# Two post-processing steps, a fetch and three orders moved in an attention and GEGLU kernel

## The chip, the cores and the metric

The kernel runs on one core of one Trainium2 chip. The metric is the device time in microseconds of one execution of the program; lower is better. Engines are called by their names in the profile: PE is TensorE (PEld its weight loads), DVE is VectorE, ACT is ScalarE, POOL is GpSimd and SP is SyncE, which here only issues DMAs.

## The reference

The input x has 2048 rows (S) of 576 columns (D); the GEGLU's inner width is 4608 (F). All data is fp32.

```python
xn = layernorm(x)
q, k, v = heads(xn @ wqkv)              # 32 heads of 18 columns
pq, pk = phi(q), phi(k)                 # where(t > 0, t + 1, exp(t)) + 1e-6
o = (pq @ (pk.T @ v)) / (pq @ sum(pk) + 1e-6)     # linear attention, no mask
s = o @ wo
h = gelu(xn @ w_gate) * (xn @ w_up)     # 2048 x 4608
out = x + s * silu(h @ w_down)
```

## The kernel before, in words

Every fp32 operand of a matmul is split into two words that TensorE takes at full rate: a high word, written by ACT as a rounding copy, and a low word, which DVE makes by subtracting the high word from the source. A product then takes three matmuls (high by high, and the two mixed ones). The large products use a Strassen-like scheme, so that fewer block products are multiplied and DVE and POOL add blocks instead. All instructions are issued in the order in which the Python program runs; nothing reorders them. The helpers `act`, `vec`, `mm`, `pool` and `dma` (lines 145 to 157) issue one instruction each, so L146 is any ACT instruction, L149 any of DVE, L152 any matmul, L155 any of POOL and L158 any DMA.

The stages are these.

- **k, v and q.** `kv_tile(t)` (line 582) makes k and v of tile t of 128 rows in three passes (`x_mm(t, 0..2)`); between them it post-processes k (`k_post`: DVE takes `e_k` and `pk` from PSUM, ACT the exponential, POOL the sum) and v (`v_post`: ACT copies to `va`), and it normalises tile t+1 for the matmuls (`place(t + 1)`: DVE subtracts `mr` from `x` and makes `xf`, ACT makes the high word `xo`, DVE the low word). Tile 8 is N0, the first of the second half of the rows; q of the rows in between is made in `q_mm` and `q_store` (ACT `e_q`, DVE `ph`, POOL the sum of both). A table of hooks names what runs beside each piece. `sort_rows(n)` transposes the layernorm statistics on PE and copies them to `mr` with one ACT instruction.
- **Attention output.** `s_mm` multiplies by the state; `den`, `scale` and `halve` make the denominators, the scaled `pq` and its words, piece by piece in a table of hooks.
- **Gate and up.** 36 matrices (18 of gate, 18 of up) of seven block products each, named al, be, ga, de, al, ga, de. `step` (line 1007) issues each product in two halves and runs the post-processing of an earlier product behind it; so the last two posts, `post_5` (reads ga) and `post_6` (reads de), are left over at the end, and `flush()` (line 1020) issues the last half product and then both. A post adds to u, stores to a spot of SBUF (`spot_g`, `spot_h`, `spot_m`) and runs what the list `todo` hangs on it; POOL adds up combinations of h from those spots (`run_events`) and they go to `hs` in DRAM. At the gate's start the x operands `B21`, `B22` and `T4` come back from DRAM by `back` on SP's queue, with the second weight matrix (`load_mat(1)`, tile `raw_1`) between.
- **Down.** 26 block products p of h words and w_down words, five units each (`UNITS`: two blocks of 128 rows of K in each, one in the last). A block is 12 matmuls of 128x288, so that a unit of two is 24. `load_unit` fetches h words from `hs` into `raw_a`, `raw_b`, `raw_h`, `raw_g`; `cut(u)` (line 1260) splits unit u: ACT writes the high word to `hi` or `beside`, DVE overwrites the raw tile with the low word. `make_words` splits w_down's block into `w_head` (five blocks of K) and `w_end` (four). `down_all` (line 1460) cuts two units ahead of the matmuls: `cut(u + 2)` stands ahead of the matmuls of unit u. The cuts of units 0 to 2 and the words of product 0 hang on the last posts (`down_first`, line 1440): `post_5` of the last up matrix carries `cut(2)` and the second half of product 0's words. The high word of unit 3 goes into the part of `hi` that unit 0's matmuls read. After a product, `read` adds its PSUM banks (`bd`) to the accumulators (`acc`); an output that is complete is closed by `close` (line 1406), per tile of 128 rows one silu on ACT, two DVE additions or products on `sx`, and a store. The list `late` of closings is worked off two a unit. The last product runs tile by tile, with `add_in` on DVE ahead of it.

```python
if u:
    cut(u + 2)
for kt in range(*UNITS[k]):
    down_mm(p, kt, range(TT))
load_unit(p + 1, k)
```

Of the kernel before, what the change touches and what calls it, by code (L numbers as in the profile page):

```python
# [16 lines left out]
P = 128  # L17
S = 2048
D = 576
# [3 lines left out]
HALF = D // 2  # L23
# [4 lines left out]
NG = DF // (2 * P)  # L28
# [28 lines left out]
NM = NG // 2  # L57

KP, TP = (1, 0, 2, 3), (3, 1, 2, 0)
# [43 lines left out]
def block_kernel(ctx, tc, x, xe, xt, wq_d, wkv_d, wo, wgu_d, wd_d, out):  # L103
    nc = tc.nc
# [473 lines left out]
    def run(todo, n=None):  # L578
        for _ in range(len(todo) if n is None else min(n, len(todo))):
            todo.pop(0)()  # L580

    def kv_tile(t, late_=(), end=()):

        ahead = t % (2 * TT) != 2 * TT - 1
        x_mm(t, 0)
        if t % 2 == 0:
            kv_pair(t)
        n0 = (t + 1) // 2 * 2
        if n0 in mixed:
            sort_rows(n0)  # L590
        if ahead:
            turn(t + 1)
        k_post(t, 0)
        x_mm(t, 1)
        if ahead:
            place(t + 1)
            save(t + 1)
        k_post(t, 1)
        v_post(t, 1)
        run(list(late_))  # L600
        x_mm(t, 2)
        run(list(end))
        v_post(t, 2)

    def kv_pair(t):

# [45 lines left out]
    at = {}  # L652
# [366 lines left out]

    def flush():  # L1020
        phase(True, begun_.pop())
        for f in posts:
            f()
        posts.clear()
# [67 lines left out]
    spots, free, place_of, left, events = [], {}, {}, {}, {}  # L1092
# [57 lines left out]
    def run_events(at):  # L1150
        for f in events.pop(at, []):
            f()
# [56 lines left out]
    def load_reg(at, nm, third=None):  # L1209
        if at not in reg:  # L1210
            b = big(REG[at], [P, ODD_W if REG[at] in ODD else REG_W], F32, f"b_{at}")
            reg[at] = b[:, 0 : KT * HALF].rearrange("p (k d) -> p k d", k=KT)
        j, c = int(nm[0]) - 1, int(nm[1]) - 1
        par, f = divmod(KP[j], 2)
        src = wd_d[par::2, :, f, c * HALF : (c + 1) * HALF].rearrange("g p d -> p g d")
        k = slice(0, KT) if third is None else slice(3 * third, 3 * third + 3)
        dma(out=reg[at][:, k], in_=src[:, k])

# [236 lines left out]
    def closings(p):  # L1455
        return [
            lambda o=o, j=j: close(o, j) for o, e in ENDS.items() if e == p for j in range(TT)
        ]

    def down_all():  # L1460
        late = []
        last = NP - 1
        for u in range(NP * NU):
            p, k = divmod(u, NU)
            n = KT * p + 2 * k
            for at in sorted(events):
                if at <= H_END + n // 2:
                    run_events(at)
            if p in LOADS and k < 3:
                load_reg(*LOADS[p], k)  # L1470
            if k == 0:
                for o, e in ENDS.items():
                    if e == p:
                        load_sx(o)
            if k < 2:
                change(p + 1, k)
                if p in SHARED:
                    make_words(p + 1, k)
            elif k < 4:
                make_words(p + 1, k - 2)  # L1480
                if p + 1 in SHARED and p:
                    make_words(p + 2, k - 2)
            if p == last and k == 0:
                read(p - 1)
                late += closings(p - 1)
            if p == last and k == 1:
                run(late, 1)
            if u:
                cut(u + 2)
            if p == last and k == 2:  # L1490
                break
            for kt in range(*UNITS[k]):
                down_mm(p, kt, range(TT))
            load_unit(p + 1, k)
            run(stores)
            if p == last:
                continue
            if k == 1 and p:
                read(p - 1)
                late += closings(p - 1)  # L1500
            else:
                run(late, 2)
        run(late)
        run(stores)
        o = next(o for o, e in ENDS.items() if e == last)
        for j in (TT - 2, TT - 1):
            add_in(o, j, last)
        for j in range(TT):
            for kt in range(UNITS[2][0], KT):
                down_mm(last, kt, (j,))  # L1510
            late += close_last(o, j, last, j >= TT - 2)
            run(late, len(late) - 1)
        run(late)
# [166 lines left out]
    def form_apart(nm):  # L1680
# [16 lines left out]
        (0, 1): [lambda: scales(N0), lambda: form("T1")],  # L1697
        (0, 2): [lambda: form_apart("T3")],
        (0, 3): [lambda: turn(N0)],
        (1, 0): [lambda: place(N0)],  # L1700
        (1, 1): [lambda: form("T2"), lambda: spread(N0 + 2, 2), lambda: scales(N0 + 2)],
    }
# [4 lines left out]
    for n in range(N0, 2 * N0):  # L1707
# [12 lines left out]
            ends.append(make_sel)  # L1720
        if n == 2 * N0 - 1:
            ends += [lambda i=i: difference(1, i) for i in range(3)]
        kv_tile(n, late_, ends)
    ahead = {
        (2, 0): [
            lambda: kv_pair(2 * N0), kv_done, lambda: q_hold(2, 7, 4), spread_sel,
# [3 lines left out]
        (2, 2): [lambda: kv_wo(0), lambda: kv_wo(1), move_rows],  # L1730
        (2, 3): [lambda: kv_wo(2), lambda: kv_wo(3)],
        (3, 0): [lambda: den(2), lambda: q_hold(3, 8, 4)],
        (3, 1): [lambda: scale(2, 0, 1), lambda: halve(2, 0, 1)],
        (3, 2): [lambda: scale(2, 2, 3), lambda: halve(2, 2, 3)],
        (3, 3): [lambda: scale(2, 4), lambda: halve(2, 4)],
    }
    for tb in (2, 3):
        for gi in range(NHG - 1):
# [41 lines left out]
    wt["last"] = sb.tile([P, 2, P], F32R, tag="small", bufs=1, name="w_last")  # L1780
    back("T3")
    run(pieces[4] + pieces[5])
    back("B21", eng=nc.sync)
    load_mat(1)
    back("B22", "T4", eng=nc.sync)
    open_spots()
    for q in range(NQ):
        g = q // 2
# [72 lines left out]
```

## Time and profile before

| | us |
|---|---|
| median of 3 runs | 1441.13 |
| lowest and highest of the runs | 1439.12, 1441.52 |
| the profiled execution, whole | 1439.22 |
| its span in the profile | 1437.5 |
| PE busy in it | 1429.8 (99%) |
| DVE busy | 1009.7 (70%) |
| ACT busy | 578.8 (40%) |
| POOL busy | 539.3 (38%) |

The span runs from the first to the last instruction of the profiled execution; 1.7 us of that execution lie outside it. Busy times are sums over the whole span; matmuls are pipelined, so that a start of one lies before the end of the one ahead. Times of rows are counted from the span's start. In the names of tiles `bd` is PSUM of down, `raw_*` the h words and then their low words, `hi` and `beside` their high words.

### The profile page before, as it was taken

The numbers are of one execution on the slowest core, as the hardware profiler recorded it, in microseconds if no ns is written. First come the engines' busy times: TensorE is split into PE (matmuls) and PEld (weight loads), VectorE is DVE, ScalarE is ACT, GpSimd is POOL, SyncE is SP. The second block draws the span as 40 slices with busy tenths as digits, with TensorE's granted clock in tenths as the row PEclk, the third lists the DMA queues.
The fourth block names the chain that finished last, engine by engine and source line by source line (L and its number), as shares of the span: only waits on it lengthen the run. The fifth ranks groups of instructions, "written<-read, shape, count | busy, mean of one in ns | idle before, by whom it ended". The sixth has DMA issues, their size and how long they took to land.

```text
span 1437.5 us, 29286 instructions
## 1 busy us (share of the span) xinstructions
PE 1429.8 (99%) x11656; PEld 1386.1 (96%) x11656; DVE 1009.7 (70%) x1519; ACT 578.8 (40%) x1249; POOL 539.3 (38%) x550
## 2 busy tenths in 40 slices
PE   9999999999999999999999999999999999999998
PEld 8989989999999999999999999999999999999998
DVE  7778667354766756566655766656678978989898
ACT  6354365333322333322333322333336455545444
POOL 3342340125756557565465755557432000000000
PEclk9999999999999999999999999999999999999999
DMA  5454105521423314233242332314289888767886
GB/s 218 169 190 163 45 21 206 193 90 57 167 85 113 119 56 169 89 122 118 73 144 75 131 116 103 128 60 162 78 291 365 260 260 254 242 194 228 284 287 224
DMA packets 120947, 228.16 MB, mean 159 GB/s; under 512 B 11658, under 2 KB 45354, under 8 KB 120170
## 3 DMA queue, kind: packets, MB, share of 16 engines
q1 hardware_dynamic: 118234, 216.13, 44.4%
q0 software_dynamic: 2432, 9.96, 1.9%
q8 instruction: 92, 1.51, 0.5%
q14 instruction: 45, 0.37, 0.1%
q10 hardware_dynamic: 144, 0.20, 0.1%
HBM read 144.93 MB, written 81.27 MB: 157 GB/s over the span
## 4 chain that ended last, share of the span: by engine, by line
PE 93%; DVE 4%; DMA 1%; ACT 1%; issue 1%; SPq 0%; POOL 0%; ACTq 0%; DVEq 0%; POOLq 0%
PE bd L152 22%; PE ga L152 17%; PE al L152 15%; PE de L152 15%; PE kv L152 8%; PE be L152 7%; PE s L152 4%; PE q L152 2%; DMA raw_h<-hs 1%; PE kv_a L152 1%; DVE xo_T L149 1%; DVE raw_h L149 0%; PE idle L152 0%; DVE w_end L149 0%; PE d L152 0%
## 5 line engine op out<-in xcount | busy, mean ns | idle before, releaser
L155 POOL TENSOR_TENSOR sums<-raw 128x256 f32<-128x256 f32 (+1 forms) x108 | 70.5, 652 | 159.2 <-DMA raw<-in_wgu_dram 132.8
L152 PE MATMUL de<-xo_T,wa 64*128 64x512 f32 x486 | 127.4, 386 | 0.0
L152 PE MATMUL de<-xr_T,wa 64*128 64x512 f32 x486 | 127.4, 386 | 0.0
L152 PE MATMUL kv<-wkv,xo_B 128*128 128x412 f32 (+2 forms) x662 | 125.0, 347 | 0.1
L152 PE MATMUL ga<-xr_T,wa 64*128 64x512 f32 x486 | 121.6, 386 | 0.0
L152 PE MATMUL ga<-xo_T,wa 64*128 64x512 f32 x486 | 121.6, 386 | 0.0
L152 PE MATMUL de<-xo_T,wb 64*128 64x512 f32 x486 | 121.6, 386 | 0.0
L152 PE MATMUL de<-xr_T,wb 64*128 64x512 f32 x486 | 121.6, 386 | 0.0
L152 PEld LDWEIGHTS kv<-wkv,xo_B 128*128 128x128 f32 x662 | 120.1, 188 | 1.5 <-ACT xo_B L146 0.7
L152 PE MATMUL bd<-w_head,hi 128*128 128x288 f32 x516 | 117.7, 294 | 0.0
L152 PE MATMUL ga<-xr_B,wb 64*128 64x512 f32 x432 | 109.5, 386 | 0.8 <-DVE spot_h L149 0.8
L152 PE MATMUL ga<-xo_B,wb 64*128 64x512 f32 x432 | 109.7, 386 | 0.0
L152 PE MATMUL al<-xr_B,wa 64*128 64x512 f32 x432 | 109.5, 386 | 0.0
L152 PE MATMUL al<-xr_B,wb 64*128 64x512 f32 x432 | 109.5, 386 | 0.0
L152 PE MATMUL al<-xo_B,wa 64*128 64x512 f32 x432 | 109.5, 386 | 0.0
L152 PE MATMUL al<-xo_B,wb 64*128 64x512 f32 x432 | 109.5, 386 | 0.0
L152 PE MATMUL be<-xr_T,wa 64*128 64x512 f32 x432 | 109.4, 386 | 0.0
L152 PE MATMUL be<-xo_T,wa 64*128 64x512 f32 x432 | 109.4, 386 | 0.0
L149 DVE TENSOR_TENSOR u<-u,be 128x512 f32<-128x512 f32 x72 | 46.3, 685 | 84.7 <-PE be L152 72.4
L146 ACT ACTIVATE hi<-raw_h 128x1024 fp32r<-128x1024 f32 x59 | 62.4, 1060 | 87.1 <-PE bd L152 59.1
L152 PEld LDWEIGHTS de<-xo_T,wa 64*128 64x128 f32 x486 | 89.4, 184 | 1.8
L152 PEld LDWEIGHTS ga<-xo_T,wa 64*128 64x128 f32 x486 | 89.4, 184 | 1.6
(300 smaller groups left out, 4749.1 us busy)
## 6 DMA issues: line engine op xcount, KB each, us to landing
raw_h<-hs SPq DMA_DIRECT2D x176, 256.0 KB
hs<-spot_h SPq DMA_DIRECT2D x92, 256.0 KB
raw<-in_wgu_dram SPq DMA_DIRECT2D x36, 640.0 KB
hs<-spot_g SPq DMA_DIRECT2D x84, 256.0 KB
b<-in_wd_dram SPq DMA_DIRECT2D x42, 432.0 KB
hs<-spot_m SPq DMA_DIRECT2D x38, 256.0 KB
raw_g<-hs SPq DMA_DIRECT2D x22, 256.0 KB
raw_a<-hs SPq DMA_DIRECT2D x20, 256.0 KB
```

The lines of the kernel that those rows point to most:

```text
L146: pin(nc.scalar.activation(*args, **kw))
L149: pin(getattr(nc.vector, op)(*args, **kw))
L152: pin(nc.tensor.matmul(*args, **kw))
L155: pin(getattr(nc.gpsimd, op)(*args, **kw))
```

## The change

Six edits, each independent of the others.

1. **Tile 8 to 9.** `kv_tile` gets an argument `turned`, set for tile 8 alone: `place(9)` and `save(9)` run ahead of `k_post(8, 0)`, not behind it. `sort_rows(N0)` gets a hook of its own behind piece (1, 2) of q. In a tile with `late_` work `v_post(t, 2)` runs ahead of the list `end`.
2. **Attention.** `scale(2, 4)` and `halve(2, 4)` move from the hook (3, 3) to (3, 1).
3. **Gate's start.** `B22` is fetched right behind `B21`, ahead of `raw_1`.
4. **Last posts.** `flush()` issues only the last half product; `post_5` and `post_6` run in `last_post()`, called in `down_all` at unit 1 behind `cut(3)`. The events of POOL due by then move with it.
5. **Closings.** One a unit, and two only in the first unit of a product whose next has no `CHANGES`.
6. **w_down** lies in DRAM as whole blocks (the host code stores it so), read with `wd_d[KP[j], c]`.

```diff
@@ kv_tile @@
-    def kv_tile(t, late_=(), end=()):
+    def kv_tile(t, late_=(), end=(), turned=False):
...
-        k_post(t, 0)
+        if not turned:
+            k_post(t, 0)
         x_mm(t, 1)
         if ahead:
             place(t + 1)
             save(t + 1)
+        if turned:
+            k_post(t, 0)
         k_post(t, 1)
         v_post(t, 1)
         run(list(late_))
         x_mm(t, 2)
-        run(list(end))
-        v_post(t, 2)
+        for f in (None, *end) if late_ else (*end, None):
+            f() if f else v_post(t, 2)
@@ flush @@
     def flush():
         phase(True, begun_.pop())
+
+    def last_post():
         for f in posts:
             f()
         posts.clear()
@@ load_reg @@
-        par, f = divmod(KP[j], 2)
-        src = wd_d[par::2, :, f, c * HALF : (c + 1) * HALF].rearrange("g p d -> p g d")
+        src = wd_d[KP[j], c]
@@ down_all @@
+    def events_to(last):
+        for at in sorted(events):
+            if at <= last:
+                run_events(at)
...
-            for at in sorted(events):
-                if at <= H_END + n // 2:
-                    run_events(at)
+            if u > 1:
+                events_to(H_END + n // 2)
...
             if u:
                 cut(u + 2)
+            if u == 1:
+                last_post()
+                events_to(H_END + n // 2)
...
             else:
-                run(late, 2)
+                run(late, 2 if k == 0 and p + 1 not in CHANGES else 1)
@@ hooks of q @@
+        (1, 2): [lambda: sort_rows(N0)],
...
-        kv_tile(n, late_, ends)
+        kv_tile(n, late_, ends, n == N0)
@@ hooks of attention @@
-        (3, 1): [lambda: scale(2, 0, 1), lambda: halve(2, 0, 1)],
+        (3, 1): [
+            lambda: scale(2, 0, 1), lambda: halve(2, 0, 1), lambda: scale(2, 4),
+            lambda: halve(2, 4),
+        ],
...
-        (3, 3): [lambda: scale(2, 4), lambda: halve(2, 4)],
+        (3, 3): [],
@@ start of gate @@
-    back("B21", eng=nc.sync)
+    back("B21", "B22", eng=nc.sync)
     load_mat(1)
-    back("B22", "T4", eng=nc.sync)
+    back("T4", eng=nc.sync)
@@ kernel @@
-    wd = B_w_down.reshape(NG, 2, P, D).transpose(0, 2, 1, 3)
+    wd = B_w_down.reshape(NM, 4, P, 2, HALF).transpose(1, 3, 2, 0, 4)
```

VectorE at the start of down, before. `raw_a` with `hi` (x2) are the cuts of units 0 and 1; the four rows with `ga_35` are `post_5`, those with `de_35` `post_6`; `raw_b10` with `beside` is `cut(2)`, with `hi` `cut(3)`, and the next `raw_a` row `cut(4)`.

```order
L149 TENSOR_TENSOR raw_a_12430<-raw_a_12430,hi_12479 128x1024 x2
L149 TENSOR_TENSOR ga_35_1_12310<-u_35_1_12327,ga_35_1_12310 128x512
L149 TENSOR_TENSOR spot_h0_3062<-spot_h0_3062,ga_35_1_12310 128x512
L149 TENSOR_TENSOR ga_35_0_12311<-u_35_0_12329,ga_35_0_12311 128x512
L149 TENSOR_TENSOR spot_g5_3072<-spot_g5_3072,ga_35_0_12311 128x512
L149 TENSOR_TENSOR raw_b10_12473<-raw_b10_12473,beside_12525 128x1024
L149 TENSOR_TENSOR w_end0_12435<-b_22_12331,w_end0_12435 128x4x288
L149 TENSOR_TENSOR de_35_1_12345<-u_35_1_12327,de_35_1_12345 128x512
L149 TENSOR_TENSOR spot_h1_3063<-spot_h1_3063,de_35_1_12345 128x512
L149 TENSOR_TENSOR de_35_0_12346<-u_35_0_12329,de_35_0_12346 128x512
L149 TENSOR_TENSOR spot_g2_3069<-spot_g2_3069,de_35_0_12346 128x512
L149 TENSOR_TENSOR raw_b10_12473<-raw_b10_12473,hi_12479 128x1024
```

And in the changed kernel:

```order
L149 TENSOR_TENSOR raw_a_12430<-raw_a_12430,hi_12479 128x1024 x2
L149 TENSOR_TENSOR raw_b10_12473<-raw_b10_12473,hi_12479 128x1024
L149 TENSOR_TENSOR ga_35_1_12310<-u_35_1_12327,ga_35_1_12310 128x512
L149 TENSOR_TENSOR spot_h0_3062<-spot_h0_3062,ga_35_1_12310 128x512
L149 TENSOR_TENSOR ga_35_0_12311<-u_35_0_12329,ga_35_0_12311 128x512
L149 TENSOR_TENSOR spot_g5_3072<-spot_g5_3072,ga_35_0_12311 128x512
L149 TENSOR_TENSOR raw_b10_12473<-raw_b10_12473,beside_12557 128x1024
L149 TENSOR_TENSOR w_end0_12435<-b_22_12331,w_end0_12435 128x4x288
L149 TENSOR_TENSOR de_35_1_12345<-u_35_1_12327,de_35_1_12345 128x512
L149 TENSOR_TENSOR spot_h1_3063<-spot_h1_3063,de_35_1_12345 128x512
L149 TENSOR_TENSOR de_35_0_12346<-u_35_0_12329,de_35_0_12346 128x512
L149 TENSOR_TENSOR spot_g2_3069<-spot_g2_3069,de_35_0_12346 128x512
```

`cut(3)` has moved from behind all eight instructions of the posts to ahead of them; everything else keeps its place, so that `cut(2)` and `w_end` stand behind `cut(3)` and the four of `post_5`. ScalarE's `hi<-raw_b` moves in the same way, ahead of `beside<-raw_b` and `w_end<-b`.

ScalarE from q to tile 9, before. `e_q1_3` is the exponential of the fourth q piece and its second step, `mr_8` the statistics that tile 8's turn to 9 subtracts, `xo_1` the high words, `e_k8` the exponential of k of tile 8.

```order
L146 ACTIVATE e_q1_2_1215<-q_1_2_1200 128x512
L146 ACTIVATE e_q1_2_1215<-e_q1_2_1215 128x512
L146 ACTIVATE e_q1_3_1237<-q_1_3_1222 128x512
L146 ACTIVATE e_q1_3_1237<-e_q1_3_1237 128x512
L146 ACTIVATE mr_8_1258<-mx_8_1045 128x512
L146 ACTIVATE xo_1_B11_1140<-xf_1_B11_1141 128x3x128
L146 ACTIVATE xo_1_B21_1143<-xf_1_B21_1144 128x3x128
L146 ACTIVATE e_k8_1261<-e_k8_1261 128x576
```

And in the changed kernel:

```order
L146 ACTIVATE e_q1_2_1215<-q_1_2_1200 128x512
L146 ACTIVATE e_q1_2_1215<-e_q1_2_1215 128x512
L146 ACTIVATE mr_8_1221<-mx_8_1045 128x512
L146 ACTIVATE e_q1_3_1239<-q_1_3_1224 128x512
L146 ACTIVATE e_q1_3_1239<-e_q1_3_1239 128x512
L146 ACTIVATE xo_1_B11_1140<-xf_1_B11_1141 128x3x128
L146 ACTIVATE xo_1_B21_1143<-xf_1_B21_1144 128x3x128
L146 ACTIVATE e_k8_1285<-e_k8_1285 128x576
```

`mr_8` has moved ahead of the two instructions of `e_q1_3`. On VectorE the two rows `e_k8` and `pk_8` of `k_post(8, 0)` have moved behind the seven rows of `x_8`, `xf_1` and `xo_1`.

SyncE's queue at the gate's start, before:

```order
L158 DMA xr_B21_3054<-kept_0_B21_692 128x2x1024
L158 DMA raw_1_3056<-in_wgu_dram 128x1280
L158 DMA xr_B22_3058<-kept_0_B22_948 128x2x1024
L158 DMA xr_T4_3060<-kept_0_T4_1407 128x2x1024
L158 DMA raw_2_3316<-in_wgu_dram 128x1280
```

And in the changed kernel:

```order
L158 DMA xr_B21_3054<-kept_0_B21_692 128x2x1024
L158 DMA xr_B22_3056<-kept_0_B22_948 128x2x1024
L158 DMA raw_1_3058<-in_wgu_dram 128x1280
L158 DMA xr_T4_3060<-kept_0_T4_1410 128x2x1024
L158 DMA raw_2_3316<-in_wgu_dram 128x1280
```

`xr_B22` and `raw_1` have changed places; `xr_T4` has as many transfers ahead of it as it had.

## Rows read from the trace of the kernel before

**Rows 1.** The page: TensorE in part 1, its granted clock by slices in part 2.

```profile
PE 1429.8 (99%) x11656; PEld 1386.1 (96%) x11656; DVE 1009.7 (70%) x1519; ACT 578.8 (40%) x1249; POOL 539.3 (38%) x550
...
PEclk9999999999999999999999999999999999999999
```

**Rows 2.** Waits of TensorE: engine, what waited <- releaser: us, times, longest.

```profile
PEld ga L152 <- DVE spot_h L149: 1.1, 1, 1.1
...
PEld bd L152 <- DVE raw_h L149: 1.1, 3, 0.4
...
PEld kv L152 <- ACT xo_B L146: 0.7, 2, 0.4
...
PEld bd L152 <- DVE raw_b L149: 0.5, 1, 0.5
...
PEld s L152 <- DVE pq L149: 0.3, 1, 0.3
...
PEld kv_a L152 <- ACT va L146: 0.2, 1, 0.2
```

**Rows 3.** Timeline of VectorE, start of down: start us, us, engine, line, op.

```profile
1061.27 0.69 DVE L149 TENSOR_TENSOR ga<-u,ga 128x512 f32<-128x512 f32 x1
...
1064.07 1.23 DVE L149 TENSOR_TENSOR raw_b<-raw_b,beside 128x1024 fp32r<-128x1024 f32 x1
...
1065.21 2.45 DVE L149 TENSOR_TENSOR w_end<-b,w_end 128x1152 fp32r<-128x1152 f32 x1
...
1070.24 1.22 DVE L149 TENSOR_TENSOR raw_b<-raw_b,hi 128x1024 fp32r<-128x1024 f32 x1
```

**Rows 4.** Timeline of ScalarE, start of down.

```profile
1065.10 1.06 ACT L146 ACTIVATE hi<-raw_b 128x1024 fp32r<-128x1024 f32 x1
```

**Rows 5.** Timeline of TensorE, start of down.

```profile
1061.27 0.53 PE L152 MATMUL bd<-w_head,hi 128*128 128x288 f32 x2
...
1067.95 0.29 PE L152 MATMUL bd<-w_head,raw_b 128*128 128x288 f32 x1
...
1069.27 0.42 PE L152 MATMUL bd<-w_end,beside 128*128 128x288 f32 x2
```

**Rows 6.** Timeline of GpSimd, start of down.

```profile
1064.86 1.59 POOL L155 TENSOR_TENSOR spot_h<-spot_g,spot_h 128x512 f32<-128x512 f32 x1
```

**Rows 7.** Groups on VectorE, 1074 to 1174 us: instruction, count, busy us, mean ns, idle.

```profile
L149 DVE TENSOR_TENSOR w_end<-b,w_end 128x1152 fp32r<-128x1152 f32 x5 | 6.8, 1352 | 0.0
```

**Rows 8.** Timeline of TensorE, first gate matrix.

```profile
290.82 0.46 PE L152 MATMUL ga<-xr_B,wb 64*128 64x512 f32 x1 [0.75 <-DVE spot_h L149]
```

**Rows 9.** Timeline of GpSimd, first gate matrix.

```profile
288.37 0.74 POOL L155 TENSOR_TENSOR sums<-raw 128x256 f32<-128x256 f32 x1 [11.85 <-DMA raw<-in_wgu_dram]
```

**Rows 10.** Timeline of ScalarE, turn of tile 8 to 9.

```profile
109.88 0.58 ACT L146 ACTIVATE e_q<-q 128x512 f32<-128x512 f32 x1
...
111.03 1.13 ACT L146 ACTIVATE mr<-mx 128x512 f32<-128x512 f32 x1
```

**Rows 11.** Timeline of VectorE, turn of tile 8 to 9.

```profile
112.19 1.39 DVE L149 TENSOR_TENSOR x<-x,mr 128x768 f32<-128x768 f32 x1
...
119.23 0.96 DVE L149 TENSOR_TENSOR x<-x,mr 128x768 f32<-128x768 f32 x1 [0.34 <-ACT mr L146]
```

**Rows 12.** Timeline of GpSimd, turn of tile 8 to 9.

```profile
110.22 2.55 POOL L155 TENSOR_TENSOR ph<-ph,e_q 128x512 f32<-128x512 f32 x2 [4.93 <-DVE ph L149]
```

**Rows 13.** Timeline of VectorE, the last product.

```profile
1423.00 0.45 DVE L149 TENSOR_TENSOR sx<-acc,sx 128x288 f32<-128x288 f32 x1
...
1423.86 1.22 DVE L149 TENSOR_TENSOR raw_h<-raw_h,hi 128x1024 fp32r<-128x1024 f32 x1
...
1428.18 0.82 DVE L149 TENSOR_TENSOR bd<-bd,acc 128x288 f32<-128x288 f32 x2
```

**Rows 14.** Timeline of TensorE, the last product.

```profile
1429.02 0.29 PE L152 MATMUL bd<-beside,hi 128*128 128x288 f32 x1
```

**Rows 15.** Chain of waits around the start of the 24th product: start us, us, what.

```profile
1379.82 8.04 DMA raw_h<-hs
```

## The prediction

> **What bounds the kernel now.** I read the page first: TensorE is busy for 1429.8 of 1437.5 us and its granted clock is at the top in every slice, the level of 2.4 GHz [rows 1]. So nothing done on another engine shortens anything; the change can only remove TensorE's waits or add some. Second come the waits of TensorE's weight loads [rows 2]. The reader is to see how little there is: 1.1 us in the first gate matrix, 0.5 at down's start, 1.1 in three places in down (0.3 to 0.4 each), 0.7 and 0.2 around tile 9, 0.3 in the attention. These rows add up to 3.9, but the half of the `xo_B` row that lies outside tile 9 is not touched, and the matmul starts lose a little less than the loads wait: I take 3.0 us for all that the six edits could regain. A measurement of this kernel can tell 0.2% from no change, 2.9 us here. The edits must therefore all work, and cost nothing, to be seen as a gain at all; one stall made elsewhere decides. So third I read the timelines where instructions move.
>
> **Down's start, the largest term.** The new place of `cut(3)` is ahead of `post_5`, and VectorE takes instructions in order. Before, VectorE begins the four `ga` instructions of `post_5` at 1061.27, `cut(2)` at 1064.07 and `w_end` at 1065.21 [rows 3]. The four therefore take 1064.07 - 1061.27 = 2.80 us, a cut 1065.21 - 1064.07 = 1.14. In the changed kernel the four wait for `cut(3)`, whose high word ScalarE starts at 1065.10 [rows 4]. Can ScalarE start it earlier? That instruction writes the part of `hi` that unit 0's matmuls read. They start at 1061.27; the blocks between 1061.27 and unit 2's first low word at 1067.95 are four of 12 matmuls and two matmuls more, 50 in 6.68 us, 0.133 each [rows 5], so unit 0's 24 end at about 1064.45. Its h words must have landed too, and ScalarE now comes to it first. Between 1064.45 and 1065.10 I take the later, the one that has a row. Then: high word done at 1066.16, `cut(3)` done 1.14 later at 1067.30, the four of `post_5` done at 1070.10, `cut(2)` at 1071.25 to 1071.4. TensorE wants that low word at 1067.95 [rows 5]: a stall of 3.3 to 3.5 us, taken as 3.5, where there was none.
>
> Behind it stands `w_end`, which took 2.45 us although the same instruction takes 1.35 on the mean later [rows 3, 7]. The difference is a GpSimd addition of 1.59 us that starts at 1064.86, ahead of it, and is over at 1066.45 [rows 6]; 1.15 later `w_end` ends. That addition reads the spot that `post_5` writes, so it moves along and meets `w_end` again. `w_end` then ends at 1071.3 + 2.45 = 1073.7, and TensorE wants it one unit-half after `cut(2)`, at 1069.27 + 3.5 = 1072.8 to 1073.0: +0.8 more. The Trainium skill, page "SBUF — State Buffer", section "SBUF: two separate sides", says that a VectorE instruction with two SBUF inputs and a GpSimd instruction that reads SBUF exclude each other, whichever starts first holding the port pair for its whole length. The 2.45 us agree with it; by that rule the 0.8 falls away if `w_end` starts first.
>
> Sum of the place: 3.5 + 0.8 = 4.3 of new stalls; the old stall behind `cut(3)`, 0.4 of the 0.5 in [rows 2], goes. **Down's start: +3.9.** Bounds: +2.2 (ScalarE at 1064.45, `w_end` in 1.35) and +4.5 (later cuts, which have under a microsecond in hand, come late as well). `post_6`, the additions that follow and the stores of h all move by about 3 us; nothing of product 0 reads them, and TensorE itself is later by more.
>
> **Tile 8 to 9.** `mr_8` takes ScalarE from 111.03 to 109.88, but the two `e_q1_3` move behind it, by the 1.1 us of `mr` [rows 10]. On VectorE `ph_1_3` waits for `e_q1_3`, so it starts at about 111.55 where it started at 110.50, and `x_8`, now right behind it, starts at 112.2, as before [rows 11]: jumping ahead of `k_post` gains what waiting for `e_q` loses. GpSimd's addition of `ph_1_3`, half of a pair of 2.55 [rows 12], now comes at 112.2 as well; the earlier pair had lengthened `x<-x,mr` from 0.96 to 1.39 [rows 11, 12]. If the 1.28 falls between `x` and `xf`, the operand is about 0.7 to 1.0 late; if not, the old stall, 0.26 of the 0.7 in [rows 2], is gone. I take **+0.7** (bounds -0.3 to +1.0), since the two start at the same time and `x` is the shorter. `k_post(8, 0)` and with it the exponential of `e_k8`, the next `mr` and `va_9` come 1.2 to 1.7 us later; TensorE already waited 0.2 there [rows 2]: **+0.3** (bounds -0.2 to +0.7).
>
> **Attention.** The stall of 0.3 on `pq` [rows 2] belongs to piece 4; two hooks earlier it has many microseconds in hand: **-0.24**.
>
> **Gate's start.** The wait put down to `spot_h` [rows 2, 8] is another: this product's first post was long done, and the weights' operand `xr_B` of that row is `B22`, which landed late. Fetched ahead of `raw_1` (on the same queue) it is there in time: **-1.0**. Cover for this: GpSimd starts on `raw_1` at 288.37 [rows 9], waits 11.85 for it, and now will be some 2 us later; these sums are for the second matrix, which begins only behind the seven products of the first. `T4` has the same transfers ahead of it, but is wanted 1 us earlier; if that is too early by a little, -0.8. If `B22`'s landing is set by the memory and not by its place, 0.
>
> **Closings.** A close takes 1423.86 - 1423.00 = 0.86 us of VectorE [rows 13]. Two of the three stalls on `raw_h` [rows 2] stand behind a pair of closes; with one the cut comes 0.86 earlier, more than either stall: **-0.65**. The third is behind an h transfer of 8.04 us [rows 15] and stays. At the end the price comes back: the closes left over push VectorE's last queue back by one, 0.86. There the `add_in` pair starts at 1428.18 and takes 0.82, half of it for the tile that TensorE begins at 1429.02 [rows 13, 14]: 1429.02 - 1428.59 = 0.43 in hand, so **+0.45** (bounds 0 and +1.0).
>
> **Wd as blocks.** The bytes and the DMA issues stay; no wait of TensorE is on `b`: **0** (bounds -0.3 and +0.3).
>
> **Sum**: 3.9 + 0.7 + 0.3 - 0.24 - 1.0 - 0.65 + 0.45 + 0 = +3.5. On the profiled execution's 1439.2 this is 1442.7. That execution lies 1.9 below the median of 1441.1, on which the forecast is put: **1444.6 us**.
>
> **Rivals.**
>
> *Not slower: GpSimd's additions never overlap at the wrong moment.* Place: `w_end` at down's start and `xf` of tile 9. Price: 0.8 + 0.7 + 0.3. It decides by which starts first: if `w_end` is issued before GpSimd's addition, and that addition of `ph` before `x` is done with, these are zero, and the sum is 3.5 - 1.8 = +1.7, 1442.8: inside 0.2%. For it: in rows 11 an `x` beside GpSimd was only 0.43 longer. Against: at down's start the order of rows 3 and 6 comes from the data and repeats.
>
> *TensorE's clock drops.* The new idle piece of 3.5 us is far longer than any here; through the 1.1 us one of [rows 8] the granted clock stayed at its top [rows 1]. Were it at the lower level of 1.2 GHz afterwards for as long as it stood idle, half of 3.5 is lost again: +1.8, 1446.4. No row here shows the lower level. The Trainium skill, page "TensorE: Matmul & The Clock Gate", section "HAM oscillation — how this bites in real kernels", has waits for data bring the engine back to the lower clock; no trace here shows it.
>
> *Everything but the minimum at down's start goes well.* +2.2 - 0.4 there, -0.3 and -0.2 at tile 9, -0.24, -1.0, -0.65, no price at the end: -0.6, 1440.5.
>
> *The fetch does nothing*: B22 lands no earlier. +1.0 on the sum: 1445.6.
>
> **How the numbers follow.** Forecast 0.55, the overlap 0.18, the clock 0.10, all well 0.12, the fetch 0.05. The forecast's own range is 1442.6 to 1446, by the bounds on down's start and the tail; 2.9 above the median is 1444.0, so two thirds of it are slower by over 0.2%. The clock is slower whole, the fetch nearly whole, the overlap case by a fifth. Together 0.36 + 0.10 + 0.04 + 0.03 = 0.53, rounded to 0.52. Faster by over 0.2% needs all of the 3.0 us and no cost: a third of the all-well case, 0.05 with the scatter of the runs. The rest, 0.43, is within. The range reaches from 1440.3, the all-well case less the scatter, to 1447.3, the clock case and a term at its bound.
>
> **What would show it.** Right: in the waits of TensorE one of about 3.5 us on `raw_b` at about 1067 us, with the four `ga` instructions of VectorE starting at 1067 and not 1061; `w_end` again near 2.45; the row `ga` on `spot_h` gone; `x<-x,mr` still at 112, counted from the same start; one or no stall on `raw_h` in the middle of down; a new small one at the last product's third tile. Wrong: if no wait over 2 us stands at down's start, the main step falls, and with it the sign; if the granted clock leaves the top there, the clock is it; if the `spot_h` row stays, the fetch is.

## The result and the profile after

| | median, us | runs | ratio to the kernel before, 95% interval |
|---|---|---|---|
| kernel before | 1441.61 | 16 | |
| changed kernel | 1444.73 | 16 | 1.0020 [1.0012, 1.0028] |

The change makes the kernel 3.1 us slower. One execution of the changed kernel, the one whose profile came with this result, took 5090 us, with its matmuls two and a half to three times as long; it tells nothing of the change, and the rows below are of another execution of the same kernel, of 1443.46 us (the first experiment).

The page of that execution, its span and TensorE's part, as in [rows 1]:

```profile
span 1441.7 us, 29278 instructions
...
PE 1430.8 (99%) x11656; PEld 1396.1 (97%) x11656; DVE 1010.8 (70%) x1519; ACT 577.8 (40%) x1249; POOL 539.7 (37%) x550
```

The span is 1441.7 - 1437.5 = 4.2 us longer than before, and TensorE's busy time grew by 1.0 of that. The rest, 3.2, went into waits, and their list says where (the view of [rows 2]):

```profile
PEld bd L152 <- DVE raw_b L149: 3.5, 1, 3.5
...
PEld kv_a L152 <- POOL va L155: 1.2, 3, 0.7
PEld kv L152 <- ACT xo_B L146: 1.2, 2, 0.9
...
PEld bd L152 <- DVE raw_h L149: 0.2, 1, 0.2
```

The reader is to see four things. One wait of 3.5 us on `raw_b` stands first; the one wait on `raw_b` before was 0.5. Around tile 9 the waits on `xo_B` and on `va` have become 0.5 us longer each (before, `va` had the 0.2 of [rows 2] and the row below). The row of the first gate matrix (`ga` on `spot_h`, 1.1) is gone, and so is that of the attention (0.3). Of the three waits on `raw_h`, 1.1 in all, 0.2 is left. The row of `va` before:

```profile
PEld kv_a L152 <- POOL va L155: 0.5, 2, 0.3
```

VectorE at down's start, which answers to [rows 3]:

```profile
1066.15 1.23 DVE L149 TENSOR_TENSOR raw_b<-raw_b,hi 128x1024 fp32r<-128x1024 f32 x1 [4.91 <-ACT hi L146]
1067.29 0.69 DVE L149 TENSOR_TENSOR ga<-u,ga 128x512 f32<-128x512 f32 x1
...
1069.95 1.22 DVE L149 TENSOR_TENSOR raw_b<-raw_b,beside 128x1024 fp32r<-128x1024 f32 x1
1071.08 2.43 DVE L149 TENSOR_TENSOR w_end<-b,w_end 128x1152 fp32r<-128x1152 f32 x1
1073.44 0.68 DVE L149 TENSOR_TENSOR de<-u,de 128x512 f32<-128x512 f32 x1
...
1089.07 1.22 DVE L149 TENSOR_TENSOR raw_b<-raw_b,hi 128x1024 fp32r<-128x1024 f32 x1
```

`cut(3)` now comes first, idle until 1066.15 because ScalarE starts on the high word at 1065.06, when the h words have landed (its row stands below). `post_5` begins at 1067.29 (1061.27 before), `cut(2)` at 1069.95 (1064.07). The last row is a cut of product 1, of which the fourth experiment speaks. ScalarE, which answers to [rows 4], and TensorE, which answers to [rows 5]:

```profile
1065.06 1.06 ACT L146 ACTIVATE hi<-raw_b 128x1024 fp32r<-128x1024 f32 x1 [5.27 <-DMA raw_b<-hs]
```

```profile
1067.58 0.42 PE L152 MATMUL bd<-w_head,beside 128*128 128x288 f32 x2
1071.22 0.61 PE L152 MATMUL bd<-w_head,raw_b 128*128 128x288 f32 x1 [3.22 <-DVE raw_b L149]
...
1073.79 0.68 PE L152 MATMUL bd<-w_end,beside 128*128 128x288 f32 x2
```

It starts unit 2's two matmuls with the high word at 1067.58, and the third, which reads the low word, at 1071.22. Then look at the steps: from 1071.22 to 1073.79 ten matmuls take 2.57 us, 0.257 each, where 0.133 is usual. The windows of TensorE over this stretch (start and end, us, busy and count of matmuls, granted clock, share of the DMA engines, GB/s):

```profile
1061.00:1067.00 6.00, 6.00 (x45) 1.00 0.92 303
1067.00:1071.20 4.20, 1.00 (x8) 0.86 0.91 362
1071.20:1076.70 5.50, 5.48 (x23) 0.50 0.98 347
1076.70:1084.00 7.30, 7.30 (x56) 0.99 0.58 212
```

The granted clock stands at 0.50, 1.2 GHz, from the end of the wait to 1076.7. So down's start costs two things: the wait, and slow matmuls behind it.

### The profile page after: what moved, and what is told of

It reads as the page before. It is cut to its first block, busy times and chain, and to the rows that moved or that the text cites. A ratio compares the mean times of both kernels' runs of the same rounds, so it can differ in the third digit from the quotient of the medians.

```text
span 5088.6 us, 29278 instructions
## 1 busy us (share of the span) xinstructions
PE 5082.6 (100%) x11656; PEld 3271.7 (64%) x11656; DVE 970.6 (19%) x1519; ACT 582.9 (11%) x1249; POOL 510.8 (10%) x550
## 4 chain that ended last, share of the span: by engine, by line
PE 100%; DVE 0%; POOL 0%; ACT 0%; issue 0%; POOLq 0%
PE bd L152 25%; PE ga L152 17%; PE al L152 16%; PE de L152 16%; PE kv L152 9%; PE be L152 7%; PE s L152 4%; PE q L152 4%; PE kv_a L152 1%; PE kw L152 0%; PE d L152 0%; PE b L152 0%; PE idle L152 0%; PE xt L269 0%; PE q L625 0%; PE ms L261 0%
## 5 line engine op out<-in xcount | busy, mean ns | idle before, releaser
L152 PE MATMUL kv<-wkv,xo_B 128*128 128x412 f32 (+2 forms) x662 | 434.7, 928 | 0.0
L152 PE MATMUL de<-xr_T,wa 64*128 64x512 f32 x486 | 428.1, 1091 | 0.0
L152 PE MATMUL de<-xo_T,wa 64*128 64x512 f32 x486 | 428.1, 1091 | 0.0
L152 PE MATMUL de<-xr_T,wb 64*128 64x512 f32 x486 | 418.6, 1092 | 0.0
L152 PE MATMUL de<-xo_T,wb 64*128 64x512 f32 x486 | 418.6, 1092 | 0.0
L152 PE MATMUL ga<-xr_T,wa 64*128 64x512 f32 x486 | 418.4, 1092 | 0.0
L152 PE MATMUL ga<-xo_T,wa 64*128 64x512 f32 x486 | 418.4, 1092 | 0.0
L152 PE MATMUL be<-xr_T,wa 64*128 64x512 f32 x432 | 374.2, 1092 | 0.0
L152 PE MATMUL be<-xo_T,wa 64*128 64x512 f32 x432 | 374.1, 1092 | 0.0
L152 PE MATMUL bd<-w_end,hi 128*128 128x288 f32 x448 | 268.6, 736 | 0.0
```

What stands on the lines that cost most here:

```text
L152: pin(nc.tensor.matmul(*args, **kw))
```

## The experiments

Where lateness is given, it is the start of the n-th matmul of down, less the start of the first, less (n - 1) times 0.1323 us, the step of TensorE where nothing waits; all from TensorE's timeline.

**1. The changed kernel again**, unaltered, for its trace.

> The changed kernel unaltered, for its trace. Theory: one wait of TensorE of 3.3 to 3.5 us at the first low word of unit 2 in down, followed by 0.8 us on w_end; the wait on B22 gone; 0.5 to 1.0 us more around tile 9 than before; one small wait in the last product; time 3.1 us above the kernel before, as in the result. Rival clock: the granted clock is at its lower level behind the long wait, and the loss at down's start is 1 to 2 us larger than the waits. Rival elsewhere: no wait over 2 us at down's start, the loss lies at tile 9 and the end.

1443.95 us, ratio 1.0013 [1.0003, 1.0023]: only 0.4 above the kernel before in this series (1443.53), where 3.1 was expected; the second experiment comes back to this. The wait at the first low word is there, 3.4 us; B22's is gone; tile 9 has 1.0 us more. Two steps came out otherwise: `w_end` is not waited for, and no wait is left in the last product. The wait on `w_end` did not vanish: it was done at 1073.44, and TensorE came to it at 1073.79 because its matmuls were slow. The rival of the clock is right on what happens.

**2. The posts put back, and the posts alone.** Edit 4 is undone in the changed kernel, or made alone in the kernel before.

```diff
 def flush():
     phase(True, begun_.pop())
-
-def last_post():
     for f in posts:
...
-if u == 1:
-    last_post()
-    events_to(H_END + n // 2)
```

> The changed kernel with edit 4 undone: both last posts run at the end of gate and up, as before; the other five edits stay. Theory: 3.9 us below the changed kernel, so about 0.8 us below the kernel before (between -1.5 and +0.3). Rival clock: 5 to 6 us below the changed kernel, 2 to 3 below the one before. Rival elsewhere: within 1 us of the changed kernel.

> The kernel before with edit 4 alone. Theory: +3.9 us on the kernel before (3.3 to 4.5). Rival clock: +5 to +6. Rival elsewhere: within 1 us of the kernel before.

Undone: 1440.51 us, 0.9986 [0.9976, 0.9995], which is 3.4 us below the changed kernel of the same series (1443.95). Alone: 1445.03, 1.0012 [1.0004, 1.0021], which is 1.5 above the kernel before and not 3.9. In its trace the wait is 3.5, `w_end` shows its own wait of 0.7, and down is late by 5.5 us at its 73rd matmul, where the kernel before is late by 0.1 (0.5 a little later). So edit 4 is the loss; the next largest, tile 9, is 1.0. But the medians show less than the traces. Undoing edit 4 gives 3.4 in the medians, and 4.1 between the profiled spans (1441.7 and 1437.6); edit 4 alone costs 1.5 in the medians, and 5.8 between the spans (1443.3 and 1437.5). The kernel before has a median of 1443.53 here, and 1441.61 in the first series. Something in the kernels without edit 4 is not the same from run to run; experiments 5 to 7 look for it.

**3. The order mended: `cut(2)` first.** Both posts stay behind `cut(3)`, but `cut(2)` and `w_end` are taken out of `post_5`.

```diff
-[lambda: load_reg("32", "32"), lambda: cut(2), lambda: make_words(0, 1)],
+[lambda: load_reg("32", "32")],
...
+if u == 1:
+    cut(2)
+    make_words(0, 1)
 if u:
     cut(u + 2)
```

> The changed kernel, but cut(2) and the second half of product 0's words are taken out of post_5 and run ahead of cut(3) and of both posts. Theory: what costs is the order on VectorE alone, so none of the waits at down's start is left: 4.3 us below the changed kernel, 1.2 below the kernel before (0.4 to 2.0). Rival elsewhere: within 1 us of the changed kernel. Third way: the posts, now 6 us later, hold up later cuts or GpSimd's sums of h; then a new wait stands in products 0 to 2.

1443.55 us, 1.0003 [0.9995, 1.0012]. My theory gave 1.2 below the kernel before; it is the third way. The long wait is gone, and the clock stays up, but there are five new waits, the longest 1.6 us, and at the 433rd matmul down is late by 5.2 us, where the changed kernel is by 5.8. VectorE's timeline says why:

```profile
1072.45 3.45 DVE L149 TENSOR_TENSOR raw_a<-raw_a,hi 128x512 fp32r<-128x512 f32 x2
1076.22 2.33 DVE L149 TENSOR_TENSOR raw_a<-raw_a,beside 128x1024 fp32r<-128x1024 f32 x1 [0.32 <-ACT beside L146]
...
1081.15 2.31 DVE L149 TENSOR_TENSOR raw_b<-raw_b,hi 128x1024 fp32r<-128x1024 f32 x1
```

The cuts of 1024 columns take 2.3 us where a cut alone takes 1.22, and one of 512 and one of 1024 take 3.45. Each of them meets an addition of GpSimd, whose timeline has these beside them:

```profile
1072.91 1.30 POOL L155 TENSOR_TENSOR spot_h<-spot_h,spot_g 128x512 f32<-128x512 f32 x1
...
1076.15 1.31 POOL L155 TENSOR_TENSOR spot_h<-spot_h,spot_m 128x512 f32<-128x512 f32 x1
...
1080.59 1.79 POOL L155 TENSOR_TENSOR spot_h<-spot_g,spot_h 128x512 f32<-128x512 f32 x1
```

1.1 us is lost on each of the longer ones. The additions hang on the posts; with the posts 6 us later they fall on the cuts of products 0 and 1, which VectorE can't afford. That they meet is read from the two timelines; no run moved the additions without the posts, so how much of the loss is theirs and how much that of the posts themselves in VectorE's queue is not shown. Edit 4 then costs 3.0 us (1443.55 against 1440.51 with the posts back) even without the order inside it: what `cut(3)` gains, 0.4, is paid for behind it.

**4. The wait filled.** What do the slow matmuls cost? 30 matmuls of no use stand between units 1 and 2 of product 0, so that TensorE works while it would wait. They share the PSUM banks of product 0, whose sums are then not the reference's.

```diff
     for kt in range(*UNITS[k]):
         down_mm(p, kt, range(TT))
+    if u == 1:
+        for i in range(FILL):  # FILL = 30
+            mm(banks[0][i % TT][:, HALF:512], hi_v[0, 1][:, 0, 0:P],
+               word[0][0][0][:, 0, 0 : 512 - HALF], start=True, stop=True, skip_group_check=True)
```

> The changed kernel with 30 matmuls of 224 columns, of no use, put between units 1 and 2 of product 0, into columns of PSUM that no product uses: about 3.2 us in which TensorE waited. Theory with the clock: the work has the same start of unit 2, the granted clock stays at the top, and the 2.4 us that the 23 matmuls behind the wait took longer are saved; w_end, hidden by them, then shows a wait of 0.4 to 0.8 us; together 1.6 to 2.0 us below the changed kernel. Rival: the slow matmuls come from something else (weights, PSUM); then the time is that of the changed kernel or up to 0.3 us more.

1443.98 us, 1.0011 [1.0002, 1.0020]: the time of the changed kernel (1443.95 in the other series). Windows and timeline of TensorE:

```profile
1067.00:1071.20 4.20, 4.04 (x36) 1.00 0.98 379
1071.20:1076.70 5.50, 4.45 (x31) 1.00 0.92 321
```

```profile
1067.27 3.50 PE L152 MATMUL bd<-w_head,hi 128*128 128x224 f32 x30
...
1071.60 0.40 PE L152 MATMUL bd<-w_head,raw_b 128*128 128x288 f32 x1 [0.56 <-DVE raw_b L149]
...
1073.96 0.40 PE L152 MATMUL bd<-w_end,beside 128*128 128x288 f32 x1 [0.65 <-DVE w_end L149]
```

The clock stays at the top, from 1076.7 to 1084 too: it was the idle piece that brought it down. At the 73rd matmul the kernel is 0.8 us less late than the changed one (5.15 for 5.99). But the saving is gone by the 217th (5.91 for 5.99): `w_end` is now waited for (0.65 idle at 1073.96), and two later cuts by 0.2 and 0.5. Theory and rival were both wrong on the time, for a reason that neither named: VectorE is nearly as late as TensorE until about 1090, and a TensorE that runs faster only waits for it. A part is chance, as `cut(3)` starts 0.4 later here (1066.53) than in the changed kernel. But that kernel's own trace sets a bound too: the cut that begins at 1089.07 is over at 1090.29, and TensorE comes to it at 1091.2, so of the 2.4 us of slow matmuls some 0.9 at most could be had: an estimate, which takes VectorE's times as they are.

**5. Tile 9, and `cut(3)` between the posts.** The first kernel has edits 1 and 4 undone; the second is the same, but with `post_6` alone behind `cut(3)`. Of the first diff two lines are shown.

```diff
...
-kv_tile(n, late_, ends, n == N0)
+kv_tile(n, late_, ends)
...
-(1, 2): [lambda: sort_rows(N0)],
```

> The changed kernel with edits 1 and 4 undone: the fetch of B22, the attention hook, the closings and w_down's blocks stay. Theory: the two waits around tile 9 are 0.26 and 0.24 us again (0.76 and 0.71 in the changed kernel), so 1.0 us below the kernel without edit 4 alone, and 1.6 us below the kernel before. Rival: the new tile order is worth more elsewhere (attention or gate start earlier), then no lower than the kernel without edit 4.

```diff
 def flush():
     phase(True, begun_.pop())
+    posts.pop(0)()
```

> The same, but cut(3) stands between post_5 and post_6 (edit 4 for post_6 alone). Theory: cut(3) comes 2.7 us earlier on VectorE, the wait of 0.4 to 0.5 us behind it goes, and nothing else is late: 0.4 us below the kernel without edits 1 and 4. Rival, after what cut(2) ahead of both posts showed: the post that is put off lengthens VectorE's queue where it has no time left (1072 to 1090 us), and a later cut waits 0.5 to 1.5 us instead.

1440.19 us, 0.9984 [0.9973, 0.9994], and 1440.56, 0.9983 [0.9973, 0.9992]. The second was expected 0.4 below the first; the medians don't show it. The waits of TensorE, first with edit 1 (experiment 2, posts back), then without:

```profile
PEld kv_a L152 <- POOL va L155: 1.2, 3, 0.7
PEld kv L152 <- ACT xo_B L146: 1.1, 2, 0.9
```

```profile
PEld kv L152 <- ACT xo_B L146: 0.7, 2, 0.4
...
PEld kv_a L152 <- POOL va L155: 0.5, 2, 0.3
```

In these rows tile 9 takes 0.7 + 0.4 less without edit 1, of which 0.2 comes back as a wait on ScalarE's `va`; the attention's first matmul starts at 209.0 and not at 210.0. The medians of the two series (1440.51 and 1440.19) differ by 0.3 and can't show it. In the kernel with `cut(3)` between the posts the wait of 0.5 behind it is gone, and two others, 0.8 and 0.5 on `raw_b`, stand at 1081 and 1085; theory and rival both have half. And the trace of the first kernel shows what may make the medians differ: one wait on `raw_a` of 2.7 us, with no counterpart in the trace of experiment 2's first kernel, which differs from it by edit 1 alone:

```profile
PEld bd L152 <- DVE raw_a L149: 2.7, 1, 2.7
```

**6. w_down's blocks alone, and the kernel before again.**

```diff
-src = wd_d[par::2, :, f, c * HALF : (c + 1) * HALF].rearrange("g p d -> p g d")
+src = wd_d[KP[j], c]
```

> The kernel before with w_down stored as blocks alone (edit 6). Theory: 0 (-0.3 to +0.3 us). Rival: fewer, longer runs free the queues at down's start, where the DMA engines are busy all the time; then h words land earlier, and it is 0.5 to 1.5 us faster.

> The kernel before, unaltered, for a second trace: its runs lie in two groups, near 1440.3 and near 1443.8. Theory, after the run without edits 1 and 4: h words of product 1 land when the DMA engines let them, VectorE's cuts of units 5 to 8 have no time in hand, and where one comes over 2 us late the granted clock drops as well. If this execution is of the upper group, its trace shows a wait of 2 us or more between 1072 and 1090 us and the lower clock behind it; if of the lower group, no such wait and the clock at the top. Rival: the upper group is spread over the whole run (a little in each stage); then no stage is more than 1 us longer.

The blocks alone: 1443.50 us, 1.0010 [0.9998, 1.0021], no gain that shows. The kernel before again: its execution took 1443.16 us, 3.9 more than the one that the prediction was made from. The whole difference is at one place. ScalarE and then TensorE:

```profile
1075.37 1.06 ACT L146 ACTIVATE hi<-raw_a 128x1024 fp32r<-128x1024 f32 x1 [7.97 <-DMA raw_a<-hs]
```

```profile
1079.36 0.40 PE L152 MATMUL bd<-w_head,raw_a 128*128 128x288 f32 x1 [2.35 <-DVE raw_a L149]
```

```profile
1076.70:1079.30 2.60, 0.31 (x2) 1.00 1.05 403
1079.30:1081.00 1.70, 1.64 (x11) 0.88 1.02 380
1081.00:1084.00 3.00, 3.00 (x14) 0.50 0.43 148
```

In the execution predicted from, ScalarE's row at this place was another:

```profile
1073.34 1.06 ACT L146 ACTIVATE hi<-raw_a 128x1024 fp32r<-128x1024 f32 x1 [6.66 <-DVE raw_a L149]
```

The view puts this wait down to VectorE, whose cut of unit 4 ended just before. But the instruction does not need that cut: in the kernel before with block 32 fetched later (experiment 7) it starts at 1069.96, ahead of the cut:

```profile
1071.71 4.51 DVE L149 TENSOR_TENSOR raw_a<-raw_a,hi 128x512 fp32r<-128x512 f32 x2
```

What is left is the landing of the first h words of product 1, in both executions. The last transfer that the instruction waits for was issued at 1064.72 and at 1064.78; its last signal comes at 1072.91 and at 1074.93, 0.44 us ahead of the instruction both times. So here the same words landed 2.0 us later. VectorE's cut then starts at 1076.46 and takes 2.85 us where 1.22 is usual, beside two additions of GpSimd (1075.70 to 1078.21):

```profile
1076.46 2.85 DVE L149 TENSOR_TENSOR raw_a<-raw_a,hi 128x1024 fp32r<-128x1024 f32 x1 [3.27 <-ACT hi L146]
```

TensorE waits 2.35 us, and behind that the granted clock falls to 0.50 until 1084. The DMA engines are busy all this time (share 1.0 in the windows); why the landing moved by 2 us stays open. Down is late by 5.1 us at the 136th matmul, where the other execution of the same kernel is late by 0.5. So in this execution the kernel before loses some 4 us at this place. Nearly all its runs lie between 1438.8 and 1446.6, with medians from 1441.5 to 1443.5 in the five series.

**7. The landing moved.** Ahead of product 1's h words SyncE issues the fetch of w_down's block 32, which product 3 needs first. It is put behind them, in the kernel with `cut(3)` between the posts, in the kernel before, and in the changed one. (The expectation calls it 432 KB; the list of DMA issues has 1296 KB.)

```diff
-[lambda: load_reg("32", "32"), lambda: cut(2), lambda: make_words(0, 1)],
+[lambda: cut(2), lambda: make_words(0, 1)],
...
     load_unit(p + 1, k)
+    if u == 4:
+        load_reg("32", "32")
```

> The kernel with cut(3) between the posts, and the fetch of w_down's block 32 (432 KB, issued ahead of the h words of product 1) put behind the h words of product 1. Theory: these h words land 1 to 2 us earlier, the waits of units 5 to 8 go, 0.5 to 1.2 us below the kernel with cut(3) between the posts, and its runs lie closer together. Rival: VectorE's and GpSimd's work sets these cuts, not the landing; then no difference.

> The kernel before with the later fetch of block 32 alone. Theory: the upper group of its runs goes, and the median falls by 1 to 2 us. Rival: both groups stay.

> The changed kernel with the later fetch of block 32. Theory: its wait at down's start comes from VectorE's order and not from a landing, so nothing is gained: 1443.5 to 1444.5 us, the wait of 3.4 us with the lower clock behind it stays; it is then 4 to 5 us above the best version, which shares that fetch and has edits 1 and 4 undone or mended (1.0 of it is tile 9), and 2 to 3 us above the kernel before with the later fetch alone. Rival: its wait is one of landing too; then it falls to 1440 to 1441.5.

| kernel with the later fetch | median, us | lowest, highest | ratio to the kernel before |
|---|---|---|---|
| with `cut(3)` between the posts, edit 1 undone | 1439.68 | 1438.64, 1442.32 | 0.9979 [0.9969, 0.9990] |
| kernel before | 1441.35 | 1440.45, 1442.92 | 0.9989 [0.9981, 0.9998] |
| changed kernel | 1445.64 | 1443.20, 1447.62 | 1.0027 [1.0013, 1.0040] |

ScalarE takes the first h words of product 1 at these times in the first two:

```profile
1069.08 1.06 ACT L146 ACTIVATE hi<-raw_a 128x1024 fp32r<-128x1024 f32 x1 [3.17 <-DMA raw_a<-hs]
```

```profile
1069.96 1.06 ACT L146 ACTIVATE hi<-raw_a 128x1024 fp32r<-128x1024 f32 x1 [2.70 <-DVE de L149]
```

That is 3.0 us earlier than in the kernel with `cut(3)` between the posts (1072.07), and 3.4 and 5.4 earlier than in the two traces of the kernel before. In the kernel before, all 12 runs are now below 1443; without the edit 14 of 29 in the same series are above. The mean granted clock of each run agrees: 1.000 in all 12, and 0.998 or 0.999 in 13 of those 14. So the late landing, with the lower clock behind it, made the upper part of its runs. The lower part is gone as well (lowest 1440.45, without the edit 1438.82), and in the trace two waits on `raw_a`, of 0.5 and 1.4 us, are new: the later fetch has a price too. In the first kernel the rival is right. Waits of 0.8 and 0.5 on `raw_b` at 1081 and 1085 stay, so those are not the landing's; the profiled spans are 1436.9 with the later fetch and 1436.7 without, and the runs lie no closer together (over 3.7 us, and 3.5 without). The changed kernel gains nothing. In it the fetch already goes out behind the first two h transfers of product 1, since it hangs on `post_5`, which edit 4 moved; in SyncE's queue three `raw_a` stand ahead of it (one transfer of product 0, two of product 1), where the kernel before has one. The kernel before, then the changed one:

```profile
1061.34 0.43 SPq L158 DMA_DIRECT2D raw_a<-hs  x1
1061.82 0.43 SPq L158 DMA_DIRECT2D b<-in_wd_dram  x1
1063.14 5.06 SPq L158 DMA_DIRECT2D raw_a<-hs  x4
```

```profile
1061.23 3.70 SPq L158 DMA_DIRECT2D raw_a<-hs  x3
1064.98 0.42 SPq L158 DMA_DIRECT2D b<-in_wd_dram  x1
```

Its wait is VectorE's order, as before:

```profile
PEld bd L152 <- DVE raw_b L149: 3.7, 1, 3.7
...
PEld bd L152 <- DVE w_end L149: 0.9, 1, 0.9
```

At 1445.64 it is above the range that I gave (1443.5 to 1444.5), and 4.3 us above the kernel before with the same fetch (5.5 by the two ratios), where I wrote 2 to 3. The profiled spans of these two are 3.4 apart (1443.2 and 1439.8). So with the later fetch in both, the change costs between 3.4 and 5.5 us; the two ran in different series, and no run says it closer. The first kernel of the table is 3.1 us below the kernel before in its series (0.21% in the ratio), and below the changed kernel; most of that it has without the later fetch too (0.9983 in experiment 5).

## Why the prediction was right, point by point

The time, its sign and its main place were right: 1444.6 forecast, 1444.73 measured. The parts were not all so, and two misses cancelled; that the sum came so close is luck.

- **Down's start, the wait.** Predicted 3.5 us on the first low word of unit 2, at 1067; measured 3.4, with `post_5` at 1067.29 (predicted 1067.30) and ScalarE's high word at 1065.06 (1065.10). The order did what was told. That the high word comes at the same time is partly luck: before, ScalarE came to it at 1065.10 behind two other instructions, and in the changed kernel it comes first and waits for the landing (with the wait filled, 1065.44).
- **Down's start, behind the wait.** Predicted 0.8 on `w_end`, which does take 2.43 us again. The step that failed is that the clock stays up: it was a rival with a chance of 0.10 and a price of 1.8. The 23 matmuls in the 5.5 us at 0.50 would take 23 x 0.1323 = 3.0 us at the top, so 2.4 went there, and in this the 0.8 was hidden. Down is late by 6.0, where 4.3 was forecast, against 0.5 (0.4 forecast) before: +5.5, and not +3.9. Filling the wait showed that this does not mean that the clock costs 2.4: with it at the top, waits for VectorE come instead, and by the estimate of experiment 4 0.9 is the most it can have cost.
- **Tile 8 to 9.** Predicted +0.7 and +0.3; measured +0.5 on `xo_B` and +0.5 on `va`, +1.0 in both. For the first the mechanism was as told. ScalarE's row of `mr` at its new place, then VectorE's, then GpSimd's, which answer to [rows 10 to 12]:

```profile
109.86 1.11 ACT L146 ACTIVATE mr<-mx 128x512 f32<-128x512 f32 x1
110.88 0.58 ACT L146 ACTIVATE e_q<-q 128x512 f32<-128x512 f32 x1
```

```profile
112.15 0.95 DVE L149 TENSOR_TENSOR x<-x,mr 128x768 f32<-128x768 f32 x1
113.13 1.99 DVE L149 TENSOR_TENSOR xf_B<-x,mr 128x384 f32<-128x384 f32 x2
```

```profile
112.37 1.88 POOL L155 TENSOR_TENSOR ph<-ph,e_q 128x512 f32<-128x512 f32 x1 [0.88 <-ACT e_q L146]
```

`x<-x,mr` starts at 112.15, as it did, and is short (0.95); the addition issued at 112.37 comes behind it, and `xf_B` waits for that: 1.99 us for two that took 1.03. The Trainium skill, page "SBUF — State Buffer", section "SBUF: two separate sides", says that the one that starts second waits for the whole of the first; the rows agree here, and in the third experiment.

- **Gate's start** (-1.0) and **attention** (-0.24): both rows are gone from the waits. The gate and up stage is 0.76 shorter, since 0.26 of small pieces came back at its first products.
- **Closings.** Predicted -0.65, with the third wait left; measured -0.9, all three gone but 0.2. The third stood behind a DMA [rows 15], and I can't say from these runs what made it shorter. Part of the -0.9 may be chance: over the traces, the waits on `raw_h` are 0.2 to 0.9 in all with this edit and 0.4 to 1.3 without, and no run has the edit alone.
- **The end.** Predicted +0.45 for the `add_in` pair; measured nothing in the changed kernel. It does appear elsewhere: 0.3 with the posts back and 0.5 to 0.6 in the kernels of experiment 5, but also 0.6 with edit 4 alone and with w_down's blocks alone, which have the closings of before. So it isn't the price of the closings alone, and this stays open.
- **w_down's blocks.** Predicted 0; 1.0010 [0.9998, 1.0021] shows no gain.
- **The base.** In the profile the sum is +4.2 (tile 9 +1.0, attention and others -0.3, gate and up -0.8, down +4.4, rounded), and not +3.5. In the medians it is +3.1. The step that failed is the one that put the sum on the median: I took the 1.9 us between the profiled execution and the median as scatter. By experiments 6 and 7 it holds a loss of up to 4 us, in down's start too, that the kernel before has in a part of its runs. The changed kernel's trace does not have it: there product 1's first h words are fetched ahead of block 32, and TensorE comes to them later. That kernel owes this to edit 4 as well, through SyncE's queue, which my account of the edit did not follow: the fetch of block 32 moved with `post_5`. So 1.1 us of the profiled difference is not seen in the medians, and the forecast met the result by a clock that it left out and a base that it took too low.

## What to carry to other kernels

Before putting work behind a cut or copy, list what else that work carries: here `post_5` carried the words of the very next unit and the start of GpSimd's additions, and saving a wait of 0.4 us cost 3.4 in the medians and 5.5 in the trace behind it. Where one engine has no time left over some 20 us, a wait removed there comes back at one of its next instructions. Look at the queue that feeds the place as well: in the kernel before, a large fetch moved behind the transfers that are needed first took 1.5 us off the median, though in the kernel with `cut(3)` between the posts it bought nothing that shows. And if repeated runs of the same kernel lie 4 us apart, take a second profile before adding up microseconds: the first one may lack the very loss that the change trades against.

## What the runs showed of the hardware that I had not expected

- TensorE's granted clock fell to 0.50 behind waits of 3.4 us (changed kernel) and of 2.35 us (kernel before, second trace), for 5.5 and about 3 us; behind the wait of 1.1 us in the first gate matrix, and those of up to 1.6 us of the third experiment, it stayed at 1.00. With the 3.4 us filled by matmuls it stayed at 1.00 too. The Trainium skill, page "TensorE: Matmul & The Clock Gate", section "HAM oscillation — how this bites in real kernels", has waits for data do this; here it happens once in a kernel that is 99% busy.
- Half the clock for 5.5 us, 2.4 us of slower matmuls, was worth 0.1 us at the 217th matmul of down (5.99 us late with it, 5.91 without) and by estimate 0.9 at most, because VectorE was late as well.
- A cut of 1.22 us on VectorE takes 2.3 beside an addition of GpSimd on SBUF, as the 2.31 and 2.33 of the third experiment show.
- With one block of 1296 KB taken from ahead of the 256 KB transfers on the same queue, in the kernel before, ScalarE had the first of them 3.4 to 5.4 us earlier (1069.96 against 1073.34 and 1075.37). Of two executions of the same kernel, with the DMA engines busy all the time, one had them 2.0 us later than the other.
